# Moving steps in the drain order of a fused window attention and MLP kernel

## The chip, the cores and the metric

The kernel runs on one core of a Trainium2 chip, as one launch. The metric is the device time of that launch in microseconds. Three runs of the kernel before took 1027.41 to 1027.53 us, with a median of 1027.45 us.

## The reference

Two stages, in float32 and float64. The first is a causal window over 7 positions whose weights come from a softmax; the second is a two-layer MLP with a SiLU between.

```python
# x: (4, 4096, 192); weight_gen: (4, 4096, 8, 7); group = 192 // 8
w = weight_gen - max(weight_gen, axis=-1); w = exp(w); w = w / (sum(w, axis=-1) + 1e-09)
x_pad = concatenate([zeros((B, 6, D)), x], axis=1)
out = einsum('bshk,bskhg->bshg', w, x_unf)       # x_unf[b, s, k] = x_pad[b, s + k], as heads of 24
# the MLP: x is out as (16384, 192), w_in (192, 2048), w_out (2048, 192), both float64
h = x @ w_in
g = h * (1.0 / (1.0 + exp(-h)))
return (g @ w_out).astype(float32)
```

## The kernel before, in words

**Tiles.** The 16384 tokens are 128 partitions by 128 rows. Four rows make a block (512 tokens): 32 blocks, b = 0 to 31. Inputs arrive by chunks: chunks 0 and 1 are one block each, chunk 2 is two blocks, chunks 3 to 9 are four blocks each. The 2048 hidden values are 8 pairs p of 256.

**What each engine does for a block.**
- Window: seven products of shifted x with a softmax weight and their sums (`prep_steps`, lines 496 to 525; a product is line 508, a sum line 514). In a folded block GpSimd makes products 0 to 3 and adds them, VectorE makes 4 to 6, and `addpool` joins the two sums. GpSimd's steps are timed by the table row `fold_p`, VectorE's by `fold_v` (block 7: `fold_1`).
- Split: ScalarE rounds the scaled result to float16 (line 481), VectorE takes the rest (line 484), so that float16 matmuls keep precision. A transposing DMA and two swapping DMAs on the queue SP put both halves into `xt` and `xu` (lines 488 to 492, 476).
- First matmul (`mm1`, line 741; folded: line 677) into pairs of PSUM banks. ScalarE applies SiLU in place (line 753) and writes the upper half of the hidden values (`upper`, line 764); VectorE writes the rest (`lower`, line 768). Only after `lower` may TensorE write those banks again.
- Second matmul (line 782, from block 6 on lines 807 and 811) into other banks, and the output: in a folded block `finish_sums` (lines 700 to 709), which is one ScalarE instruction (line 705), a wide add (line 706) and a small add (line 707) on GpSimd, and for every second row tile a store on SP.

**Folding.** From block 7 on (`FOLD`), half of the first matmul is replaced by seven smaller products on sums of rows (`fold_x`, lines 616 to 643: four small GpSimd steps, ScalarE's and VectorE's halves, one transposing DMA and two swaps) and on differences of the weights (`fold_w`, lines 588 to 614: made once; five pairs of an upper half on ScalarE, line 604, and a lower half on VectorE, line 608). The partial products are put together in PSUM by `keep` on ScalarE (line 693) and four `joined` on VectorE (line 698).

**Once per chunk.** `softmax_steps` (lines 398 to 427): maximum, subtraction, exp, sum (line 416), reciprocal (lines 420 and 421), product. `scale_steps` (lines 429 to 451): sizes of four parts on ScalarE, two DMAs, then on VectorE a reduction over 512 values (line 206) and three instructions on one value a row (`small`, lines 212 and 221), then three more (`finish_scales`, `out_scale`).

**What sets the order.** The order of the instructions of each engine is written out by hand, and each engine works through its own in that order. Around the matmuls the other steps wait in a list `todo` with a due time; `drain(u)` (line 877) issues all with a due time up to u, in the order of due times. A block is 16 units. The due times are rows of the table `START`, added to a base `u0` that for block b is 16(b - 2), and for a chunk the same of its first block. Before folding a drain stands at each unit or so. In the folded loop (lines 1141 to 1177) a half block is 8 units and has drains at 0, 1, 2, 3, 5, 6 and 7 only. In short:

```python
drain(u); fold_1(x); fold_1(y); words(last); keep(); lower(last); joined x 3
drain(u + 1); tile_sums; finish_sums; plain(z); fold_2(x)
drain(u + 2); joined(3, 1, 1); drain(u + 3); tile_sums; words(z); lower(z)
drain(u + 5); fold_3(x); words(x); lower(x)
drain(u + 6); words(y); tile_sums; finish_sums; plain(last); lower(y); drain(u + 7)
```

`words` is SiLU and `upper` on ScalarE; x, y, z and last are pairs of hidden values. `fold_1(x)` needs the `lower` of the x before it, `fold_1(y)` that of the y before it, and `fold_3` the last `joined`.

Of the kernel before, what the change touches and what calls it, by code (L numbers as in the profile page):

```python
# [43 lines left out]
BESIDE = ()  # L44
START = {
    "b2v": (13.1,) * 1 + (13.2,) + (13.3,) * 3 + (13.4,) * 4 + (13.45,) + (19,) + (21,) * 2 + (23, 23, 23),
    "first_s": (-2, 1, 4, 6.2, 6.5, 8.5),
    "first_x": (-4, -1, 1, 9, 9.25, 18, 19, 20),
    "any_s": (-32, -32, -23, -15, -14, -10),
    "c4s": (-32, -32, -19, -16, -13, -10),  # L50
    "any_x": (-39, -31, -13, -5.5, -4.0, 13.5, 13.5, 15),
    "early": (-5, -41),
    "b3v": (11, 11, 13, 13, 15, 17, 17, 18, 19, 20.5, 20.5, 21, 21, 22.5, 23, 23),
    "b4v": (10, 12, 13, 14.5, 16, 17, 18.5, 20, 22.5, 23, 23),
    "any_p": (11.25,) * 5,
    "any_v": (11, 11.5, 13, 14, 15, 17, 18.5, 20, 22.5, 23, 23),
    "fold_1": (9, 9, 11, 13, 14, 14, 14, 19, 19),
    "fold_v": (5, 7, 9, 11, 12.5, 14.5, 17, 19, 19),
    "fold_p": (0.5, 3.5, 5, 7, 9, 11, 14),
    "fold_s": (14.5, 16.5, 16.5, 16.5, 18, 23, 23),  # L60
    "fold_w": (36, 58, 60, 62, 66, 81, 81, 84, 86, 87, 88, 90, 93, 94, 95),
    "prep": (12.5,),
    "load": (0,),
}
# [1159 lines left out]
```

## Time and profile before

| | |
|---|---|
| profiled execution, its own time | 1027.18 us |
| its span, first to last instruction | 1025.4 us |
| TensorE matmuls (PE) busy | 1011.7 us, 99% |
| VectorE (DVE) busy | 851.7 us, 83% |
| ScalarE (ACT) busy | 823.6 us, 80% |
| GpSimd (POOL) busy | 627.6 us, 61% |
| granted TensorE clock | 1.000 over the span |
| share of PE in the chain that ended last | 90% |

Busy is the time in which an engine worked on at least one instruction. Matmuls overlap one another, so PE busy is no measure of how fast it goes. The folded part begins at 234 us. A row of a timeline gives the start and the length in us, engine, line, operation, what it writes and reads, and in brackets how long the engine had been idle and what ended that.

### The profile page before, as it was taken

The numbers are of one execution on the slowest core, as the hardware profiler recorded it, in microseconds if no ns is written. First come the engines' busy times: TensorE is split into PE (matmuls) and PEld (weight loads), VectorE is DVE, ScalarE is ACT, GpSimd is POOL, SyncE is SP. The second block draws the span as 40 slices with busy tenths as digits, with TensorE's granted clock in tenths as the row PEclk, the third lists the DMA queues.
The fourth block names the chain that finished last, engine by engine and source line by source line (L and its number), as shares of the span: only waits on it lengthen the run. The fifth ranks groups of instructions, "written<-read, shape, count | busy, mean of one in ns | idle before, by whom it ended". The sixth has DMA issues, their size and how long they took to land.

```text
span 1025.4 us, 32480 instructions
## 1 busy us (share of the span) xinstructions
PE 1011.7 (99%) x14392; PEld 732.4 (71%) x14392; DVE 851.7 (83%) x905; ACT 823.6 (80%) x875; POOL 627.6 (61%) x525
## 2 busy tenths in 40 slices
PE   9999999999999999999999999999999999999998
PEld 7699777677777766677667776677666776666666
DVE  8898877978898888889889889888888988889553
ACT  7988668767898779877898878988789878778774
POOL 1000553555887777786687677887687876777220
PEclk9999999999999999999999999999999999999999
DMA  9542511225213352124432143233422321223200
GB/s 247 157 130 73 167 33 48 58 53 170 49 40 76 61 171 59 46 53 111 121 69 58 47 153 69 61 68 63 142 54 68 71 68 45 47 54 67 63 17 25
DMA packets 105351, 82.91 MB, mean 81 GB/s; under 512 B 79869, under 2 KB 94842, under 8 KB 104186
## 3 DMA queue, kind: packets, MB, share of 16 engines
q1 hardware_dynamic: 105210, 80.84, 31.3%
q8 instruction: 112, 1.84, 0.8%
q14 instruction: 29, 0.24, 0.1%
HBM read 29.68 MB, written 12.60 MB: 41 GB/s over the span
## 4 chain that ended last, share of the span: by engine, by line
PE 90%; DVE 6%; ACT 2%; issue 1%; DMA 0%; DVEq 0%; ACTq 0%
PE banks L741 26%; PE banks L807 24%; PE banks L677 16%; PE banks L811 12%; PE banks L782 6%; PE banks L732 2%; PE banks L794 2%; DVE ringed L768 2%; DVE banks L698 1%; ACT banks L753 1%; ACT ringed L764 1%; DVE pr L508 1%; PE banks L555 1%; DVE ws L416 1%; DVE xv L698 0%
## 5 line engine op out<-in xcount | busy, mean ns | idle before, releaser
L807 PE MATMUL banks<-wo,ringed 64*128 64x384 f16 x3312 | 419.8, 322 | 0.0
L811 PE MATMUL banks<-wo,ringed 64*128 64x192 f16 x3312 | 407.7, 243 | 0.1
L768 DVE SCALAR_TENSOR_TENSOR ringed<-banks,gup,ringed 128x1024 f16<-128x1024 f32 x248 | 315.9, 1277 | 68.3 <-ACT ringed L764 68.2
L753 ACT ACTIVATE banks<-banks,inv 128x1024 f32<-128x1024 f32 x248 | 269.1, 1085 | 97.6 <-PE banks L741 81.2
L764 ACT ACTIVATE ringed<-banks,gup 128x1024 f16<-128x1024 f32 x248 | 276.1, 1113 | 8.0
L508 POOL TENSOR_TENSOR pr<-xc,wc 128x768 f32<-128x768 f32 x109 | 192.0, 1764 | 91.4 <-DVE wc L424 58.9
L807 PEld LDWEIGHTS <-ringed 64*128 64x128 f16 x3312 | 177.8, 94 | 89.3
L741 PEld LDWEIGHTS <-w 64*128 64x128 f16 x2664 | 149.9, 94 | 114.9 <-issue 4.8
L706 POOL TENSOR_TENSOR v_in<-v_in 128x384 f32<-128x384 f32 x100 | 106.1, 1061 | 193.9 <-ACT v_in L705 193.9
L741 PE MATMUL banks<-xt,w 64*128 64x512 f16 x1332 | 185.0, 376 | 3.5 <-DVE ringed L768 3.3
L741 PE MATMUL banks<-xu,w 64*128 64x512 f16 x1332 | 184.9, 376 | 0.0
L811 PEld LDWEIGHTS <-ringed 64*128 64x128 f16 x3312 | 177.7, 94 | 6.3 <-DVE ringed L768 0.4
L514 POOL TENSOR_TENSOR pr<-pr,pr 128x768 f32<-128x768 f32 x81 | 177.2, 2188 | 6.3
L698 DVE TENSOR_TENSOR banks<-banks,xv 128x512 f32<-128x512 f32 x150 | 104.0, 694 | 80.2 <-PE banks L677 74.7
L508 DVE TENSOR_TENSOR pr<-xc,wc 128x768 f32<-128x768 f32 x108 | 150.6, 1398 | 0.2
L705 ACT ACTIVATE v_in<-banks,od 128x768 f32<-128x768 f32 x100 | 89.6, 896 | 70.1 <-PE banks L811 54.2
L677 PE MATMUL banks<-xu,w 64*128 64x256 f16 (+1 forms) x600 | 135.0, 322 | 3.5 <-DVE ringed L768 3.5
L677 PE MATMUL banks<-xt,w 64*128 64x256 f16 (+1 forms) x600 | 135.0, 322 | 0.0
L677 PEld LDWEIGHTS <-w 64*128 64x128 f16 x1500 | 103.9, 94 | 29.5
L514 DVE TENSOR_TENSOR pr<-pr,pr 128x768 f32<-128x768 f32 x105 | 120.2, 1145 | 0.6
L677 PEld LDWEIGHTS <-v_in 64*128 64x128 f16 x1200 | 86.3, 94 | 27.6 <-issue 6.3
L677 PE MATMUL banks<-v_out,v_in 64*128 64x256 f16 x900 | 99.3, 269 | 0.0
(122 smaller groups left out, 960.6 us busy)
## 6 DMA issues: line engine op xcount, KB each, us to landing
xc<-in_x_dram SPq DMA_DIRECT2D x7, 2112.0 KB, 9.6
xu<-xt SPq DMA_DIRECT2D x62, 192.0 KB, 2.9
out_dram<-o SPq DMA_DIRECT2D x61, 192.0 KB, 1.9
v_out<-v_out SPq DMA_DIRECT2D x50, 128.0 KB, 2.3
wc<-in_weight_gen_dram SPq DMA_DIRECT2D x7, 448.0 KB, 3.7
ringed<-in_moe_w_out_dram SPq DMA_DIRECT2D x8, 384.0 KB, 8.7
ringed<-in_moe_w_in_dram SPq DMA_DIRECT2D x14, 192.0 KB, 8.4
ml_x<-line_x SPq DMA_DIRECT2D x7, 256.0 KB, 4.1
```

The costliest lines, as they stand in the source:

```text
L508: eng.tensor_tensor(out=pr[k].rearrange("p t (h g) -> p (t h) g", g=G), in0=xin, in1=wv, op=ALU.mult)
L514: eng.tensor_tensor(out=pr[k], in0=pr[k], in1=pr[l], op=ALU.add)
L677: nc.tensor.matmul(h, w, x, start=start, stop=False, skip_group_check=True)
L698: nc.vector.tensor_tensor(out=to, in0=quarter[:, :, in0], in1=kept[:, :, in1], op=ALU.add)
L705: nc.scalar.activation(out=s, in_=banks[:, 4:6, 0:2 * D], func=AF.Copy, scale=sc[c, "od"])
L706: nc.gpsimd.tensor_tensor(out=s[:, 0], in0=s[:, 0], in1=s[:, 1], op=ALU.add)
L741: nc.tensor.matmul(h[:, i], w16[rows, part, p, g], x_in[rows, :, k, :], start=n == 0, stop=n == NT9 - 1)
L753: nc.scalar.activation(out=h, in_=h, func=AF.Silu, scale=sc[chunk_of[b], "inv"])
L764: nc.scalar.activation(out=g_t[b, p][:, 0], in_=h_t[b, p], func=AF.Copy, scale=sc[chunk_of[b], "gup"])
L768: nc.vector.scalar_tensor_tensor(out=g[:, 1], in0=h_t.pop((b, p)), scalar=sc[chunk_of[b], "gup"], in1=g[:, 0], op0=ALU.mult, op1=ALU.subtract)
L807: nc.tensor.matmul(acc_t[b, t, i], gh_t[b, f][rows, t * P:(t + 1) * P], wo16[rows, place(f)], start=f == 0, stop=False, skip_group_check=True)
L811: nc.tensor.matmul(acc_t[b, t, i][:, 0, :], gl_t[b, f][rows, t * P:(t + 1) * P], wo16[rows, place(f), 0], start=False, stop=False, skip_gr ...
```

## The change

Nine rows of the table `START` get other numbers; no instruction is added or taken away, and no other line changes.

```diff
-    "first_s": (-2, 1, 4, 6.2, 6.5, 8.5),
-    "first_x": (-4, -1, 1, 9, 9.25, 18, 19, 20),
-    "any_s": (-32, -32, -23, -15, -14, -10),
-    "c4s": (-32, -32, -19, -16, -13, -10),
-    "any_x": (-39, -31, -13, -5.5, -4.0, 13.5, 13.5, 15),
+    "first_s": (-2, 0, 4, 5.2, 7.5, 8.5),
+    "first_x": (-9, -1, 2, 9, 9.25, 18, 19, 20),
+    "any_s": (-32, -32, -23, -16, -14, -10),
+    "c4s": (-32, -31, -19, -16, -13, -10),
+    "any_x": (-39, -31, -13, -5.5, -4.0, 12.5, 12.5, 15.5),
...
-    "fold_1": (9, 9, 11, 13, 14, 14, 14, 19, 19),
+    "fold_1": (9, 9, 11, 13, 14, 14, 14, 20, 20),
...
-    "fold_p": (0.5, 3.5, 5, 7, 9, 11, 14),
-    "fold_s": (14.5, 16.5, 16.5, 16.5, 18, 23, 23),
-    "fold_w": (36, 58, 60, 62, 66, 81, 81, 84, 86, 87, 88, 90, 93, 94, 95),
+    "fold_p": (0.5, 3.5, 5, 7, 9, 9, 14),
+    "fold_s": (14.5, 16.5, 16.5, 16.5, 18, 23, 25),
+    "fold_w": (36, 58, 60, 62, 66, 81, 81, 84, 86, 87, 87, 87, 94.5, 94.5, 95),
```

What becomes of the order in which the engines get their instructions:
- `any_x` (chunks 4 to 9): on VectorE the reduction and `small` go from behind the `lower` of x in a second half block to ahead of the sum that stands before that `lower`; the last chain of the scale goes from the last drain of a half block to the first of the next. For chunk 4 the same swap with a sum falls just before the folded part.
- `any_s` (chunks 5 to 9): the softmax sum goes from behind three `joined` to ahead of the `lower` of last.
- `fold_p` (blocks 9 to 31): GpSimd's fourth product goes from behind the two adds of `finish_sums` to ahead of them, in 23 second half blocks.
- `fold_s`: the transposing DMA of the row sums and its two swaps go from the last drain of a first half block to the second drain of the second half block.
- `fold_w`: of the conversions of the weight sums, the third lower half goes ahead of VectorE's split of block 6, the fourth behind the `lower` of pair 7 of block 5; ScalarE's fourth upper half goes up to the third, and its fifth behind the split of block 7.
- `first_s`, `first_x`, `c4s`, `fold_1`: steps of chunks 3 and 4 and the end of block 7's split, by one drain or by a place within one.

## Rows read from the trace of the kernel before

**Rows 1.** Waits of PE: who waited, for whom, us, times, longest

```profile
PE banks L677 <- DVE ringed L768: 3.5, 5, 0.7
PE banks L741 <- DVE ringed L768: 3.3, 4, 2.1
PE banks L677 <- DVE banks L698: 1.1, 5, 0.2
```

**Rows 2.** Timeline of PE: first matmuls of half blocks, and the late group at 358.64

```profile
295.44 0.27 PE L677 MATMUL banks<-xt,w 64*128 64x256 f16 x1
...
311.16 0.27 PE L677 MATMUL banks<-xt,w 64*128 64x256 f16 x1
...
341.79 0.27 PE L677 MATMUL banks<-xt,w 64*128 64x256 f16 x1
...
357.10 0.27 PE L677 MATMUL banks<-xt,w 64*128 64x256 f16 x1
...
358.64 0.27 PE L677 MATMUL banks<-xu,w 64*128 64x256 f16 x1 [0.71 <-DVE ringed L768]
...
373.31 0.27 PE L677 MATMUL banks<-xt,w 64*128 64x256 f16 x1
```

**Rows 3.** Timeline of VectorE, second half block before a chunk boundary

```profile
347.75 0.95 DVE L514 TENSOR_TENSOR pr<-pr,pr 128x768 f32<-128x768 f32 x1
...
350.44 2.10 DVE L508 TENSOR_TENSOR pr<-xc,wc 128x768 f32<-128x768 f32 x1
352.46 1.27 DVE L768 SCALAR_TENSOR_TENSOR ringed<-banks,gup,ringed 128x1024 f16<-128x1024 f32 x1
353.66 1.37 DVE L514 TENSOR_TENSOR pr<-pr,pr 128x768 f32<-128x768 f32 x1
354.95 1.27 DVE L768 SCALAR_TENSOR_TENSOR ringed<-banks,gup,ringed 128x1024 f16<-128x1024 f32 x1
356.14 0.67 DVE L206 TENSOR_REDUCE ra_x<-ml_x 128x1 f32<-128x512 f32 x1
...
357.30 1.28 DVE L768 SCALAR_TENSOR_TENSOR ringed<-banks,gup,ringed 128x1024 f16<-128x1024 f32 x1
```

**Rows 4.** Timeline of GpSimd in the same half block

```profile
346.00 1.80 POOL L514 TENSOR_TENSOR pr<-pr,pr 128x768 f32<-128x768 f32 x1
...
349.63 0.60 POOL L707 TENSOR_TENSOR o<-v_in 128x192 f32<-128x192 f32 x1
350.19 1.54 POOL L508 TENSOR_TENSOR pr<-xc,wc 128x768 f32<-128x768 f32 x1
351.80 2.41 POOL L514 TENSOR_TENSOR pr<-pr,pr 128x768 f32<-128x768 f32 x1
357.01 0.99 POOL L706 TENSOR_TENSOR v_in<-v_in 128x384 f32<-128x384 f32 x1 [2.80 <-ACT v_in L705]
```

**Rows 5.** Timeline of ScalarE in the same half block: the `upper` of y

```profile
355.03 1.11 ACT L764 ACTIVATE ringed<-banks,gup 128x1024 f16<-128x1024 f32 x1
```

**Rows 6.** Timeline of VectorE, first half block with a softmax sum

```profile
297.94 1.28 DVE L768 SCALAR_TENSOR_TENSOR ringed<-banks,gup,ringed 128x1024 f16<-128x1024 f32 x1 [0.76 <-ACT ringed L764]
...
301.26 1.08 DVE L416 TENSOR_REDUCE ws<-wc 128x128 f32<-128x896 f32 x1
```

**Rows 7.** Busy time by windows, the stretch before folding: length, then each engine

```profile
195.00:210.20 15.20, 12.12 (x198) 8.81 (x194) 14.95 (x14) 9.86 (x12) 9.17 (x8) 1.00 0.26 71
```

**Rows 8.** Timeline of PE, late first matmuls in that stretch

```profile
202.97 0.39 PE L741 MATMUL banks<-xt,w 64*128 64x512 f16 x2 [2.06 <-DVE ringed L768]
...
210.20 0.39 PE L741 MATMUL banks<-xt,w 64*128 64x512 f16 x2 [0.66 <-DVE ringed L768]
```

**Rows 9.** Timeline of VectorE in that stretch

```profile
192.84 0.62 DVE L841 SCALAR_TENSOR_TENSOR o<-banks,od,t 128x384 f32<-128x384 f32 x1 [1.00 <-ACT t L840]
...
195.69 1.32 DVE L608 SCALAR_TENSOR_TENSOR v_in<-v_out,w_up,v_in 64x256 f16<-64x256 f32 x1
...
205.42 0.48 DVE L608 SCALAR_TENSOR_TENSOR v_in<-v_out,w_up,v_in 64x256 f16<-64x256 f32 x1
```

## The prediction

> **What bounds the kernel now.** I read the list of waits first, then the order of time on TensorE, then the engines around each wait. The page has PE busy for 99% of the span, so time can come only from moments in which PE stands still, or from a new one. The list of waits has three kinds after the start-up [rows 1]: 3.5 us in five waits of the folded matmuls (line 677) for a `lower` of VectorE (line 768), 1.1 us in five waits for a `joined` (line 698), and 3.3 us in four waits of the plain first matmul (line 741) for a `lower`. Five, five and a cluster: the fives are once per chunk.
>
> The idle times are too small as a measure, because matmuls overlap. The starts of half blocks tell more [rows 2]: 357.10 - 341.79 = 15.31 us in an ordinary one, but 373.31 - 357.10 = 16.21 us after the second half before a chunk boundary, and 311.16 - 295.44 = 15.72 us where the wait for `joined` lies. So the idle 0.71 us costs 0.90 and the idle 0.22 us costs 0.41. Five of each: 6.5 us. The second matmul group of `fold_1` would have started at 358.64 - 0.90 = 357.74 [rows 2].
>
> For the cluster, the row of a window shows who is the bound: from 195.0 to 210.2 us VectorE is busy 14.95 of 15.20 us while PE falls to 12.12 [rows 7]. The waits are 2.06 at 202.97 and 0.66 at 210.20 [rows 8]; the other two of the four are 3.3 - 2.7 = 0.6 in sum.
>
> **The change part by part.**
>
> *Scale of the next chunk (`any_x`, 13.5 to 12.5).* The reduction and three small instructions (`top`, `small`) stand on VectorE between the `lower` of x (354.95) and that of y (357.30), so they push the latter by 357.30 - 356.14 = 1.16 us [rows 3]. After the change they stand ahead of the sum at 353.66. VectorE has no idle time from 350.44 on, so this move by itself saves nothing of the 1.16 us; what it changes is whom the sum meets. That sum took 1.37 us against 0.95 for the same size at 347.75 [rows 3], since GpSimd's add (351.80 to 354.21) was still running [rows 4]; 1.16 us later it is alone: 0.42 us saved. The end of the chain for the chunk (15 to 15.5) goes from the last drain of one half block to the first of the next; nothing of VectorE lies between, so its order is the same: nothing.
>
> *GpSimd's fourth product (`fold_p`, 11 to 9).* It goes ahead of the two adds of `finish_sums`, 23 times. First how the two engines disturb each other. The product at 350.44 on VectorE took 2.10, 1.15 over 0.95; GpSimd's product (350.19, 1.54) still had 1.29 to run. GpSimd's add at 351.80 took 2.41, 0.61 over the 1.80 at 346.00; VectorE's product had 0.74 to run. The sum at 353.66 took 0.42 more, with 0.55 left of GpSimd's add [rows 3, 4]. So the second to start waits for the first to end, less 0.13 us, three times alike; the `lower`s (1.27 and 1.28) are not touched.
> Now the half block at the boundary with the new order. The product starts after 346.00 + 1.80 + 0.08 = 347.88; VectorE's sum runs until 348.70, so it is 0.82 - 0.13 = 0.69 longer and ends at 347.88 + 1.54 + 0.69 = 350.11. The wide add (0.99 alone, the row at 357.01) runs from there to 351.10. VectorE's product at 350.44 waits 0.66 - 0.13 = 0.53 and ends at 351.92 instead of 352.54: 0.62 saved. GpSimd's small add (0.60) waits behind it to 352.39, and the last add (1.80) ends at 354.15, before the sum begins at 354.19. So: `lower` of z 351.84 to 353.11, the reduction and small ones to 354.19, sum to 355.14, `lower` of x to 356.33, `lower` of y to 357.53 (each starts 0.08 before the one ahead ends, as in rows 3; ScalarE's half of y is there at 355.03 + 1.11 = 356.14 [rows 5]). The release took 0.06 (358.58 to 358.64), so PE may go at 357.59, and wants to at 357.74. The 0.90 us vanish with 0.15 to spare: 5 x 0.90 = **4.5 us**. Bounds: 0.42 x 5 = 2.1 if only the sum is spared, 4.5 above. Late next is nothing in that half: `lower` of x ends 0.77 before the 357.10 at which x is wanted. In the other 18 second halves VectorE only gets earlier, and the adds that go later feed the output store alone.
> The Trainium skill (SBUF — State Buffer, § Who interferes with whom) says that the pair of ports which the two engines share is an exclusive lock, and that the loser "fully blocks". The rows say the same but for the 0.13. By the rule in full, GpSimd's product ends at 350.24, VectorE's at 352.14, the last add at 354.50, and the `lower` of y lets PE go at 357.90: 0.16 late, 0.8 us over five chunks, so the sum would be 0.8 smaller and the time 1019.6. I take the rows.
>
> *Sum of the softmax (`any_s`, -15 to -16), five chunks.* The reduction of 1.08 us (301.26) goes ahead of the `lower` at 297.94, before which VectorE idles 0.76 us for ScalarE [rows 6]. So that `lower` and the joins behind it are up to 1.08 - 0.76 = 0.32 later, and what stands ahead of the late `joined` is 0.76 us less. It was 0.41 us late: gone, with about 0.35 to spare. 5 x 0.41 = **2.0 us**; bounds 0 (if the 0.32 hits the plain matmul that waits for the same `lower`) and 2.05.
>
> *Weight sums' conversions (`fold_w`).* The lower half at 195.69 (1.32 us) goes ahead of the split of block 6, before the idle 1.00 us at 192.84; the one at 205.42 (0.48) goes behind the `lower` that PE waits for at 210.20 [rows 8, 9]. That takes 1.32 + 0.48 = 1.80 us out of the stretch in which VectorE is the bound. The two products behind the first then start earlier and meet GpSimd's terms at other points, which I can't place to better than some tenths; for that I add 0.3: **2.1 us**. Bounds: 0, if the moved conversion pushes the two output steps behind it by as much as it took, and 4.0, all of the 3.3 idle with some 0.18 more for each of the four, as the folded wait showed. ScalarE's upper halves move with them; no wait of PE names ScalarE [rows 1], so they are priced at nothing, and inside the bounds just given.
>
> *The rest.* `first_s`, `first_x` and `c4s` move the third chunk's subtraction, its sum and two of ScalarE's sizes by one place, in blocks 1 and 2, well before the cluster. Outside the cluster line 741 waits for at most the 0.6 us left over above, so the `lower`s there have slack and the price is nothing; if it weren't covered, two steps of some 1.08 (the row of the reduction, [rows 6]): 2.2 us lost. `fold_s` (23 to 25) issues a transposing DMA and two swaps one half block's edge later, but on SP they have the same neighbours (output store ahead, next output store behind), and the sums they feed are read half a block later: nothing. `fold_1` likewise keeps its order on VectorE and SP.
>
> Sum: 4.5 + 2.0 + 2.1 = 8.6 us. The profiled execution took 1027.18 (span 1025.4 and 1.8 around it), so 1018.6; the median of the runs is 0.27 above it: **1018.8 us**.
>
> **Rivals.** (B) *The waits at the boundary only shorten.* GpSimd's adds move onto VectorE's product, and it stays at 2.10: then 2.1 + 2.0 + 2.1 = 6.2 us, 1021.2. For it: three of GpSimd's instructions now crowd into 350.1 to 354.2; against: VectorE's product started second before too, and with more left ahead of it.
> (C) *The cluster gives nothing*, because the 1.00 us gap is taken by the split meeting GpSimd's add: 4.5 + 2.0 = 6.5 us, 1020.9.
> (D) *Slower: GpSimd keeps its place in front.* If both adds of `finish_sums` and the last add all go ahead of VectorE's product, it ends at 350.11 + 0.99 + 0.08 + 0.60 + 1.80 + 0.82 = 354.4 instead of 352.54. An ordinary second half has 1.16 - 0.90 = 0.26 us of slack, so it decides from a product of 2.36 us on; at 354.4 each of 18 loses 1.86 - 0.26 = 1.6 us, the five at boundaries 1.86 - 0.42 = 1.4 more than now. 28.8 + 7.2 - 4.1 = +32 us: 1059. Against it: the last add let VectorE's waiting product go first (350.44 before 351.80).
> (E) *Nothing that counts moves.* The work of VectorE ahead of each late `lower` is the same but for contention, and if the overlaps come back elsewhere the time stays: 1027.4.
>
> **How the numbers follow.** Forecast 0.57, B 0.15, C 0.14, E 0.07, D (or a small loss of that kind) 0.07. A measurement of this kernel can tell about 0.2%, 2.1 us. Faster takes forecast, B and C: 0.86; same is E: 0.07; slower is D: 0.07. The range goes from 1017.0, close to the case in which the cluster gives all of its 4.0, to 1022.5, past B and C and most of what an uncovered third chunk adds; B and C together (1023.3) stay outside.
>
> **What would show it.** Half blocks all at 15.31 us, also those of 16.21 and 15.72, with no wait on line 677; VectorE's product at 1.4 to 1.6 instead of 2.10 in 23 second halves and the sum behind it at 0.95; the 2.06 us wait at 203 us mostly gone. A product of 2.4 or more, or waits of line 677 in ordinary second halves, would make the forecast wrong, as would new waits of line 741 in blocks 1 and 2.

## The result, and the profile after

The changed kernel takes 1018.75 us (median of 4 runs, 1018.70 to 1018.76) against 1027.49 us for the kernel before in the same comparison (4 runs, 1027.41 to 1027.54). The ratio is 0.9915 with a 95% interval of 0.9898 to 0.9932: 8.74 us, or 0.85%, faster. The forecast was 1018.8. The span of the profiled execution fell by 8.4 us (1025.4 to 1017.0). The granted clock is 1.00 in both profiled executions, which is the 2.4 GHz level, so these 8.4 us are work and waits alone. The other 0.3 us are clock, as e5 shows.

The list of what PE waited for comes first again (who waited and for whom, us in total, times, longest). It answers to [rows 1].

```profile
PE banks L741 <- DVE ringed L768: 1.0, 3, 0.4
PE banks L907 <- DVE zero L893: 1.0, 1, 1.0
PE banks L570 <- DVE ringed L564: 0.7, 1, 0.7
```

The five waits of line 677 for a `lower` and the five for a `joined` are gone, and the 3.3 us of line 741 are 1.0. So is a wait of 0.2 us for line 841 (at 232.28) that [rows 1] does not show. The other two rows are from the start-up. The timeline of PE shows it by periods, the answer to [rows 2]: the starts of half blocks in the first two chunks that are folded.

```profile
293.44 0.27 PE L677 MATMUL banks<-xt,w 64*128 64x256 f16 x1
308.76 0.27 PE L677 MATMUL banks<-xt,w 64*128 64x256 f16 x1
...
339.38 0.27 PE L677 MATMUL banks<-xt,w 64*128 64x256 f16 x1
354.69 0.27 PE L677 MATMUL banks<-xt,w 64*128 64x256 f16 x1
370.01 0.27 PE L677 MATMUL banks<-xt,w 64*128 64x256 f16 x1
```

308.76 - 293.44, 354.69 - 339.38 and 370.01 - 354.69 are 15.31 to 15.32 us each, where before there were three lengths, 15.72, 15.31 and 16.21. All others of the folded part take 15.31 us too, except its first (15.53). So PE now sets the pace there.

The half block that ends at a chunk boundary, on VectorE (start, length, line, operation), answers to [rows 3]; between the reduction and the sum lie small instructions only.

```profile
348.02 1.44 DVE L508 TENSOR_TENSOR pr<-xc,wc 128x768 f32<-128x768 f32 x1
349.38 1.27 DVE L768 SCALAR_TENSOR_TENSOR ringed<-banks,gup,ringed 128x1024 f16<-128x1024 f32 x1
350.57 0.67 DVE L206 TENSOR_REDUCE ra_x<-ml_x 128x1 f32<-128x512 f32 x1
...
351.74 0.94 DVE L514 TENSOR_TENSOR pr<-pr,pr 128x768 f32<-128x768 f32 x1
352.59 2.47 DVE L768 SCALAR_TENSOR_TENSOR ringed<-banks,gup,ringed 128x1024 f16<-128x1024 f32 x2
```

And GpSimd in the same stretch, which answers to [rows 4]:

```profile
345.47 2.22 POOL L508 TENSOR_TENSOR pr<-xc,wc 128x768 f32<-128x768 f32 x1
347.65 0.99 POOL L706 TENSOR_TENSOR v_in<-v_in 128x384 f32<-128x384 f32 x1
348.72 1.18 POOL L707 TENSOR_TENSOR o<-v_in 128x192 f32<-128x192 f32 x1
349.87 1.81 POOL L514 TENSOR_TENSOR pr<-pr,pr 128x768 f32<-128x768 f32 x1
```

The product is 1.44 us instead of 2.10; the sum is 0.94 instead of 1.37, since GpSimd's last add ends at 349.87 + 1.81 = 351.68, just before it begins. The `lower` of y ends at 352.59 + 2.47 = 355.06. PE wants it at 354.69 + 0.64 (358.64 - 0.90 - 357.10 in [rows 2]) = 355.33; with the release of 0.06, 0.2 us are to spare.

In the stretch before folding the order of VectorE reads as follows, from the moved conversion on (for [rows 9]).

```profile
190.76 0.48 DVE L608 SCALAR_TENSOR_TENSOR v_in<-v_out,w_up,v_in 64x256 f16<-64x256 f32 x1
191.28 2.46 DVE L484 SCALAR_TENSOR_TENSOR xs<-pr,xup,xs 128x768 f16<-128x768 f32 x1
...
195.91 4.24 DVE L508 TENSOR_TENSOR pr<-xc,wc 128x768 f32<-128x768 f32 x2
```

GpSimd there:

```profile
187.69 3.22 POOL L508 TENSOR_TENSOR pr<-xc,wc 128x768 f32<-128x768 f32 x2 [18.04 <-DVE pr L514]
190.99 1.93 POOL L514 TENSOR_TENSOR pr<-pr,pr 128x768 f32<-128x768 f32 x1
```

The first matmuls of PE that were late before [rows 8]; the idle time before one stands in brackets. The second answers to one at 205.44 that waited 0.36 us.

```profile
201.40 0.39 PE L741 MATMUL banks<-xt,w 64*128 64x512 f16 x2 [0.29 <-DVE ringed L768]
203.62 0.39 PE L741 MATMUL banks<-xt,w 64*128 64x512 f16 x2
208.16 0.39 PE L741 MATMUL banks<-xt,w 64*128 64x512 f16 x2 [0.44 <-DVE ringed L768]
```

And the window of the same length (length, then PE, PEld, VectorE, ScalarE and GpSimd busy, the granted clock, DMA share, GB/s), which answers to [rows 7].

```profile
193.00:208.20 15.20, 14.27 (x218) 10.27 (x216) 15.03 (x14) 10.33 (x13) 11.87 (x8) 1.00 0.40 96
```

VectorE is as full as before (15.03 of 15.20), but PE does 14.27 us of work in the window instead of 12.12. The matmul that began at 210.20 now begins at 208.16, 2.04 us earlier, of which 0.11 were there ahead of this stretch (the late matmul at 184.97 is at 184.86).

### The profile page after: what moved, and what is told of

Read it like the earlier page. It is cut to its first block, busy times and chain, and to the rows that moved or that the text cites. A ratio compares the mean times of both kernels' runs of the same rounds, so it can differ in the third digit from the quotient of the medians.

```text
span 1017.0 us, 32485 instructions
## 1 busy us (share of the span) xinstructions
PE 1011.0 (99%) x14392; PEld 710.2 (70%) x14392; DVE 849.2 (84%) x905; ACT 822.2 (81%) x875; POOL 638.6 (63%) x525
## 3 DMA queue, kind: packets, MB, share of 16 engines
q8 instruction: 112, 1.84, 0.8%
## 4 chain that ended last, share of the span: by engine, by line
PE 96%; DVE 2%; ACT 1%; issue 1%; DVEq 0%; ACTq 0%
PE banks L741 27%; PE banks L807 26%; PE banks L677 18%; PE banks L811 13%; PE banks L782 6%; PE banks L732 2%; PE banks L794 2%; DVE ringed L768 1%; DVE pr L508 1%; PE banks L555 1%; PE banks L907 1%; ACT banks L753 0%; ACT ringed L764 0%; DVE pr L514 0%; PE banks L820 0%
## 5 line engine op out<-in xcount | busy, mean ns | idle before, releaser
L508 POOL TENSOR_TENSOR pr<-xc,wc 128x768 f32<-128x768 f32 x109 | 208.2, 1912 | 93.9 <-DVE wc L424 57.9
L807 PEld LDWEIGHTS <-ringed 64*128 64x128 f16 x3312 | 162.0, 94 | 104.6
L706 POOL TENSOR_TENSOR v_in<-v_in 128x384 f32<-128x384 f32 x100 | 99.4, 994 | 180.8 <-ACT v_in L705 180.8
L811 PEld LDWEIGHTS <-ringed 64*128 64x128 f16 x3312 | 161.8, 94 | 7.7 <-DVE ringed L768 0.5
L514 POOL TENSOR_TENSOR pr<-pr,pr 128x768 f32<-128x768 f32 x81 | 162.2, 2002 | 4.5
L508 DVE TENSOR_TENSOR pr<-xc,wc 128x768 f32<-128x768 f32 x108 | 136.2, 1265 | 0.2
L514 DVE TENSOR_TENSOR pr<-pr,pr 128x768 f32<-128x768 f32 x105 | 130.5, 1243 | 0.7
L707 POOL TENSOR_TENSOR o<-v_in 128x192 f32<-128x192 f32 x100 | 95.0, 950 | 7.8
```

The lines of the kernel that those rows point to most:

```text
L508: eng.tensor_tensor(out=pr[k].rearrange("p t (h g) -> p (t h) g", g=G), in0=xin, in1=wv, op=ALU.mult)
L514: eng.tensor_tensor(out=pr[k], in0=pr[k], in1=pr[l], op=ALU.add)
L706: nc.gpsimd.tensor_tensor(out=s[:, 0], in0=s[:, 0], in1=s[:, 1], op=ALU.add)
L707: nc.gpsimd.tensor_tensor(out=o[:, t], in0=s[:, 0, 0:D], in1=s[:, 0, D:2 * D], op=ALU.add)
L807: nc.tensor.matmul(acc_t[b, t, i], gh_t[b, f][rows, t * P:(t + 1) * P], wo16[rows, place(f)], start=f == 0, stop=False, skip_group_check=True)
L811: nc.tensor.matmul(acc_t[b, t, i][:, 0, :], gl_t[b, f][rows, t * P:(t + 1) * P], wo16[rows, place(f), 0], start=False, stop=False, skip_gr ...
```

## The experiments

The theory: three independent gains. **Boundary** (`any_x` with `fold_p`): in the five half blocks before a chunk boundary VectorE meets GpSimd for less long, 4.5 us. **Sum** (`any_s`): the softmax sum runs in idle time, 2.0 us. **Conversions** (`fold_w`): 1.8 us of VectorE's work leave the stretch in which it is the bound, 2.1 us. The rest: nothing. The rivals are those of the prediction, and in addition that the two rows of the boundary each give their own part, whether or not the other is there. Each edit is to the kernel before unless it says otherwise.

**The scale alone (e1).**

```diff
-    "any_x": (-39, -31, -13, -5.5, -4.0, 13.5, 13.5, 15),
+    "any_x": (-39, -31, -13, -5.5, -4.0, 12.5, 12.5, 15.5),
```

> The kernel before with the row any_x alone changed (the reduction of the next scale ahead of VectorE's sum). Theory, the two engines take turns: VectorE's work ahead of the late lower stays the same, only the sum is spared GpSimd's add (0.42 us), so each of the five boundaries is still 0.48 us late: half blocks of 15.79 instead of 16.21, 2.1 us gained, 1025.4. Rival, the place alone decides: the lower of y is free of the 1.16 us, all of 5 x 0.90 goes, 1023.0. Rival, only contention by the product counts: 1027.5.

Measured: 1025.22 us against 1027.47, ratio 0.9979 (0.9970 to 0.9988): 2.25 us. In its VectorE rows the product is as long as before and the sum is free of GpSimd:

```profile
350.83 2.11 DVE L508 TENSOR_TENSOR pr<-xc,wc 128x768 f32<-128x768 f32 x1
...
355.22 0.94 DVE L514 TENSOR_TENSOR pr<-pr,pr 128x768 f32<-128x768 f32 x1
```

The boundary half block takes 15.78 us (16.21 before), and PE still waits there, less long:

```profile
358.60 0.27 PE L677 MATMUL banks<-xu,w 64*128 64x256 f16 x1 [0.27 <-DVE ringed L768]
```

So 0.43 us come off the sum five times, the lower bound of the boundary term.

**The fourth product alone (e2).**

```diff
-    "fold_p": (0.5, 3.5, 5, 7, 9, 11, 14),
+    "fold_p": (0.5, 3.5, 5, 7, 9, 9, 14),
```

> The kernel before with the row fold_p alone changed (GpSimd's fourth product ahead of the two output adds). Theory of turns: VectorE's product falls from 2.10 to 1.44, but the sum two places later now begins 0.7 us into GpSimd's last add and waits for it, 1.93 instead of 1.37, so the lower of y comes only about 0.1 earlier: 0.3 to 0.5 us over five boundaries, 1027.1. Rival, the parts add up: 0.62 us at each boundary, 3.1 us, 1024.4. Rival, it costs: stalls in the 18 ordinary second halves, over 1028.

Measured: 1026.93 us against 1027.47, ratio 0.9995 (0.9986 to 1.0004): not told apart from nothing. The product on VectorE is shorter by 0.67, and the sum behind it longer by 0.56 (1.93 for 1.37):

```profile
350.75 1.44 DVE L508 TENSOR_TENSOR pr<-xc,wc 128x768 f32<-128x768 f32 x1
...
353.31 1.93 DVE L514 TENSOR_TENSOR pr<-pr,pr 128x768 f32<-128x768 f32 x1
```

GpSimd's last add tells why. It used to go beside the `lower`, and now begins 0.70 before the sum and has 1.12 left when the sum starts:

```profile
352.61 1.82 POOL L514 TENSOR_TENSOR pr<-pr,pr 128x768 f32<-128x768 f32 x1
```

The contention was moved from one instruction to the next. The five waits of line 677 for a `lower` are 3.0 us in all instead of 3.5, which fits the small gain expected, though the times can't confirm it. The rival by which each row brings its own part (1024.4) falls.

**Both (e3).** The edits of e1 and e2 together.

> The kernel before with any_x and fold_p changed together. Theory of turns: together they clear the five boundaries, 4.5 us, 1023.0, more than the sum of the two alone (2.1 + 0.4). Rival, additive parts: 2.1 + 3.1, cut at 4.5, also 1023.0, but then the second run alone is at 1024.4.

Measured: 1023.03 us, ratio 0.9958 (0.9944 to 0.9973): 4.44 us, where e1 and e2 add up to 2.79. No wait of line 677 for a `lower` is left; the two other kinds are untouched:

```profile
PE banks L741 <- DVE ringed L768: 3.3, 4, 2.1
PE banks L677 <- DVE banks L698: 1.1, 5, 0.2
```

**Without the fourth product (e4).** This kernel leaves GpSimd's fourth product and the sum that adds it out of the folded blocks, so that term is missing from its output. The two lines added put all later lines two further on (770 is 768).

```diff
         pool = ...
+        if fold:
+            pool[5:] = [lambda: None] * 2
```

> The kernel before without GpSimd's fourth product and its sum in all folded blocks (the output lacks that term); no step is moved. Theory of turns: VectorE's product takes 0.95 instead of 2.10 and the sum 0.95 instead of 1.37, 1.57 us saved where 0.90 is late, so the five boundaries are clear: 1023.0. Rival, the place of the reduction decides and GpSimd is no cause: 1027.5.

Measured: 1020.98 us, ratio 0.9939 (0.9922 to 0.9955): 6.5 us, 2 more than expected. The boundary is as expected: product and sum on VectorE at their undisturbed length, and no wait of the folded matmuls for a `lower`.

```profile
348.66 0.95 DVE L508 TENSOR_TENSOR pr<-xc,wc 128x768 f32<-128x768 f32 x1
...
350.86 0.95 DVE L514 TENSOR_TENSOR pr<-pr,pr 128x768 f32<-128x768 f32 x1
```

Most of the other 2 us comes from the stretch before folding, since the first folded matmul starts at 232.25 us instead of 234.03. The terms of block 7 are computed there, also without the fourth, and VectorE's two products at 197.01 meet less of it, 3.35 us in place of the 4.70 of the kernel before. Line 741, here 743, waits 1.6 us in all instead of 3.3:

```profile
197.01 3.35 DVE L508 TENSOR_TENSOR pr<-xc,wc 128x768 f32<-128x768 f32 x2
```

```profile
PE banks L743 <- DVE ringed L770: 1.6, 3, 0.7
```

I had overlooked that the edit reaches there. What it shows is that contention makes up some 1.35 us of that cluster too. The rival by which GpSimd is no cause (1027.5) falls.

**The softmax sum alone (e5).**

```diff
-    "any_s": (-32, -32, -23, -15, -14, -10),
+    "any_s": (-32, -32, -23, -16, -14, -10),
```

> The kernel before with the row any_s alone changed (the softmax sum ahead of the lower of last, five chunks). Theory: half blocks of 15.72 become 15.31, 2.0 us, 1025.4. Rival, the sum delays the lower that the plain matmul waits for: no gain or a loss, 1027.5 to 1029.

Measured: 1025.58 us against 1027.42, ratio 0.9982 (0.9972 to 0.9991): 1.84 us. The half blocks of 15.72 us are 15.31, and the wait for a `joined` is gone from the list:

```profile
PE banks L677 <- DVE ringed L768: 3.6, 5, 0.7
PE banks L741 <- DVE ringed L768: 2.3, 2, 2.1
```

Line 741 has two waits here, where [rows 1] has four. The reason is TensorE's clock: in this execution it fell to its lower level, 1.2 GHz, for 3.4 us after PE had stood still for 2.06 us at 203 (a window as in [rows 7]; 0.50 is the granted clock).

```profile
203.40:206.80 3.40, 3.40 (x19) 1.45 (x17) 3.34 (x4) 0.16 (x1) 0.00 (x0) 0.50 0.22 77
```

PE was then later itself and did not have to wait for the next two `lower`s. In the profiled execution of the kernel before, the clock in that window is 1.00. Of the 25 runs of the kernel before that e5 to e8 are compared with, 15 have a mean clock of 1.000 and a median of 1027.20 us, and 10 have 0.998 and 1027.50; so the fall costs some 0.3 us. Of the 44 runs of e1, e2, e3, e5 and e7, which keep the wait of 2.06 us, 21 have 0.998. Of the 27 runs of e4, e6, e8, e9 and the changed kernel, in which it is shorter, none has. No run changes that wait alone, so that it brings the fall is likely, not shown.

**The conversions alone (e6).**

```diff
-    "fold_w": (36, 58, 60, 62, 66, 81, 81, 84, 86, 87, 88, 90, 93, 94, 95),
+    "fold_w": (36, 58, 60, 62, 66, 81, 81, 84, 86, 87, 87, 87, 94.5, 94.5, 95),
```

> The kernel before with the row fold_w alone changed (two lower halves of the weight sums out of the stretch from 195 to 210 us). Theory: 1.9 to 2.1 us, 1025.5, the wait of 2.06 us at 203 us falls to some 0.3. Rival, the gain before folding came from the other moved rows: 1027.5.

Measured: 1025.29 us against 1027.42, ratio 0.9979 (0.9970 to 0.9989): 2.13 us. The waits of line 741 fall to what the changed kernel has, the others stay:

```profile
PE banks L677 <- DVE ringed L768: 3.6, 5, 0.7
PE banks L677 <- DVE banks L698: 1.1, 5, 0.2
PE banks L741 <- DVE ringed L768: 1.0, 3, 0.4
```

**All the other rows (e7).**

```diff
-    "first_s": (-2, 1, 4, 6.2, 6.5, 8.5),
-    "first_x": (-4, -1, 1, 9, 9.25, 18, 19, 20),
+    "first_s": (-2, 0, 4, 5.2, 7.5, 8.5),
+    "first_x": (-9, -1, 2, 9, 9.25, 18, 19, 20),
-    "c4s": (-32, -32, -19, -16, -13, -10),
+    "c4s": (-32, -31, -19, -16, -13, -10),
-    "fold_1": (9, 9, 11, 13, 14, 14, 14, 19, 19),
+    "fold_1": (9, 9, 11, 13, 14, 14, 14, 20, 20),
-    "fold_s": (14.5, 16.5, 16.5, 16.5, 18, 23, 23),
+    "fold_s": (14.5, 16.5, 16.5, 16.5, 18, 23, 25),
```

> The kernel before with first_s, first_x, c4s, fold_1 and fold_s changed. Theory: nothing, 1027.3 to 1027.6. Rival, they carry part of the gain before folding: up to 2 us, 1025.5.

Measured: 1027.17 us against 1027.42, ratio 0.9997 (0.9988 to 1.0007), with the same three kinds of waits as before. The four parts, each by itself, add up to 4.44 + 1.84 + 2.13 + 0.25 = 8.66 us, against 8.74 for the whole: within the noise they don't depend on each other.

**Two more steps out of the cluster (e8), an edit to the changed kernel.** Three waits of line 741 are left, 0.26 at 184.86, 0.29 at 201.40 and 0.44 at 208.16. The softmax sum of the `c4s` row stands ahead of the first on VectorE, and two sums of terms (2.02 us from 204.88) stand right ahead of the `lower` for which the last one waits. I moved the softmax sum ahead of a product, a `lower` and a sum, and the second of the two sums behind that `lower`.

```diff
-    "c4s": (-32, -31, -19, -16, -13, -10),
+    "c4s": (-32, -31, -19, -18, -13, -10),
-    "fold_1": (9, 9, 11, 13, 14, 14, 14, 20, 20),
+    "fold_1": (9, 9, 11, 13, 14, 14.4, 17, 20, 20),
```

> The changed kernel with two more moves on the late lowers that are left: the fourth chunk's softmax sum two places up (c4s -16 to -18), into an idle 1.86 us of VectorE at 175 us, and the last sum and the upper half of block 7 behind the lower that TensorE waits for at 208 us (fold_1: 14, 14 to 14.4, 17). Theory, VectorE's work ahead of a late lower is the price: 0.43 us at 185 and 0.62 us at 208, 1.0 us, 1017.7. Rival, the next lower is late instead: 1018.8 or more.

Measured: 1020.04 us against 1027.42, ratio 0.9927 (0.9913 to 0.9942): 1.3 us slower than the changed kernel, where 1 us less was expected. The waits at 185 and 208 are gone, but line 741 waits anew at 205.06 (0.36) and 227.05 (0.25), and a new kind stands in the list, for the output steps of line 841:

```profile
PE banks L782 <- DVE o L841: 1.6, 2, 1.1
```

GpSimd's wait for block 7's terms ends with a sum of VectorE on `pr` (line 514). With the softmax sum out of the way that sum begins at 186.21 instead of 186.71, and GpSimd at 187.18 instead of 187.69. Its add now comes ahead of the moved conversion:

```profile
190.49 1.81 POOL L514 TENSOR_TENSOR pr<-pr,pr 128x768 f32<-128x768 f32 x1
```

```profile
190.79 1.79 DVE L608 SCALAR_TENSOR_TENSOR v_in<-v_out,w_up,v_in 64x256 f16<-64x256 f32 x1
192.61 2.40 DVE L484 SCALAR_TENSOR_TENSOR xs<-pr,xup,xs 128x768 f16<-128x768 f32 x1
```

The conversion takes 1.79 us instead of 0.48, and the two output steps behind the split come too late for PE.

**Only the second of the two (e9), an edit to the changed kernel.** It tells whether the new waits of e8 came from the earlier start of GpSimd or from the `fold_1` row.

```diff
-    "fold_1": (9, 9, 11, 13, 14, 14, 14, 20, 20),
+    "fold_1": (9, 9, 11, 13, 14, 14.4, 17, 20, 20),
```

> The changed kernel with one of the two further moves: the last sum of block 7 and ScalarE's upper half of it behind the lower that TensorE waits for at 208 us (fold_1: 14, 14 to 14.4, 17); the softmax sum of the fourth chunk stays. Theory: the new waits of the run before came from GpSimd starting 0.5 us earlier on its terms of block 7, not from this move; so here the 0.44 us wait at 208 us goes and nothing comes: some 0.6 us, 1018.1. Rival, this move made the new waits at 195 and 197 us: 1020.

Measured: 1018.84 us (5 runs, 1018.76 to 1019.49) against 1027.49, ratio 0.9917 (0.9904 to 0.9931): the same as the changed kernel, where 0.65 less was expected. The two waits of line 782 aren't there, so in e8 they needed the edit of `c4s`, which is the one that lets GpSimd start earlier; that edit was not run alone. The wait at 208 is gone as expected, but another has come in the next block (and one of 0.2 us for line 841, as the kernel before has it):

```profile
225.90 0.39 PE L741 MATMUL banks<-xt,w 64*128 64x512 f16 x2 [0.49 <-DVE ringed L768]
```

VectorE's product of block 8, 0.95 us long in the changed kernel (at 222.79), starts 0.39 us behind GpSimd's add and takes 2.56:

```profile
222.09 2.56 DVE L508 TENSOR_TENSOR pr<-xc,wc 128x768 f32<-128x768 f32 x1
```

```profile
221.70 2.14 POOL L514 TENSOR_TENSOR pr<-pr,pr 128x768 f32<-128x768 f32 x1
```

GpSimd comes later than in the changed kernel because the moved sum does: its small steps of line 624 wait for that sum's `pr`, and its products of block 8 stand behind them and start at 210.25 instead of 209.01.

None of the versions run is faster than the changed kernel.

## Why the prediction was right, point by point

**The total, 8.6 us predicted, 8.74 measured.** Between the two profiled executions it is 1027.18 - 1018.75 = 8.43 us. The first folded matmul starts at 231.98 instead of 234.03, so 2.05 us lie ahead of the folded part (predicted 2.1) and 6.4 in it (predicted 6.5). The forecast then added 0.27 us, by which the median of the kernel before lay above its profiled execution. That fits the 0.3 us of the clock's fall (e5), which none of the changed kernel's four runs shows: their median and their profiled execution are both 1018.75. So a gain 0.17 too large and an addition 0.27 too large nearly cancel. That the forecast came within some tenths is its mechanism; that it came within 0.05 is luck.

**The measure.** The prediction counted 0.90 and 0.41 us per half block from periods, not the 0.71 and 0.22 of idle time. Clearing the five boundary waits gave 4.44 us (e3), where five times 0.90 is 4.5 and five times the idle time would be 3.5. Clearing the five joins gave 1.84 (e5), where five times 0.41 is 2.05 and five times 0.22 would be 1.1. Periods were the right measure both times. The 0.41 was read from one half block; the other four of its kind take 15.69 us, so the five are late by 0.41 + 4 x 0.38 = 1.93.

**The boundary, 4.5 us predicted, 4.44 measured.** The step that moves the scale "by itself saves nothing of the 1.16 us; what it changes is whom the sum meets": e1 shows it, with the lower bound of 2.1 us as 2.25. The shorter product was to bring the rest. e2 shows that it can't alone: without the 1.16 us of small instructions ahead of the sum, GpSimd's last add runs into the sum. Together product and sum are 0.66 + 0.43 = 1.09 us shorter, of which PE can use 0.90. That leaves 0.2, where the prediction had 0.15.

**The rule of the two engines.** The prediction had the second to start wait for the first to end, less 0.13 us, read from three rows; it gave 1.48 us for the product, and 1.44 came. With the changed kernel's own rows, the wide add has 347.65 + 0.99 - 348.02 = 0.62 left when the product starts, so the rule in full gives 0.95 + 0.62 = 1.57, and less 0.13 it is 1.44. The new rows carry it further: in e2 the sum has 1.12 us of the add ahead, so 0.95 + 1.12 - 0.13 = 1.94, measured 1.93; in e9 the product has 221.70 + 2.14 - 222.09 = 1.75 ahead, so 2.57, measured 2.56. The Trainium skill (SBUF — State Buffer, § Who interferes with whom) has the loser blocked fully, by which the forecast was 1019.6; the product of 1.44 us stands on the side of the rows. In that forecast the 352.14 is 0.04 too small beside its own 350.24 + 0.99 + 0.95 = 352.18, which makes it 1019.8.

**The miss.** The list of what would show it says "the sum behind it at 0.95" in 23 second halves. That holds in the five boundary halves only. In the other 18 the scale's steps are not there, and it is longer than the 1.37 us of before. In an ordinary second half of the changed kernel VectorE's product and sum are

```profile
317.40 1.45 DVE L508 TENSOR_TENSOR pr<-xc,wc 128x768 f32<-128x768 f32 x1
...
319.96 1.93 DVE L514 TENSOR_TENSOR pr<-pr,pr 128x768 f32<-128x768 f32 x1
```

and GpSimd's last add is

```profile
319.25 1.82 POOL L514 TENSOR_TENSOR pr<-pr,pr 128x768 f32<-128x768 f32 x1
```

The add has 319.25 + 1.82 - 319.96 = 1.11 us left, so the rule that the prediction already had gives 1.93. It worked the sum out for the boundary half and took it over to the others ("In the other 18 second halves VectorE only gets earlier"). It cost nothing: 0.66 saved on the product and 0.56 lost on the sum leave VectorE 0.1 us earlier still, and an ordinary half has slack.

**The softmax sum, 2.0 predicted, 1.84 measured.** The sum runs where VectorE had idled for ScalarE, and the `lower` behind it starts 296.07 - 293.44 = 2.63 us into the half block instead of 297.94 - 295.44 = 2.50: 0.13 later, within the 0.32 that the prediction allowed. There is now more slack than it counted, since VectorE idles 0.88 us for PE before the next join:

```profile
295.08 1.07 DVE L416 TENSOR_REDUCE ws<-wc 128x128 f32<-128x896 f32 x1
296.07 1.27 DVE L768 SCALAR_TENSOR_TENSOR ringed<-banks,gup,ringed 128x1024 f16<-128x1024 f32 x1
...
301.48 0.70 DVE L698 TENSOR_TENSOR banks<-banks,xv 128x512 f32<-128x512 f32 x1 [0.88 <-PE banks L677]
```

**The conversions, 2.1 predicted, 2.13 measured**, or 1027.20 - 1025.29 = 1.91 among runs with a clock of 1.000. But the parts are not as the prediction had them. The conversion that moves ahead of the split shrank from 1.32 to 0.48, while the split grew from 1.10 to 2.46, because it now meets GpSimd's add (190.99). That is what rival C describes, and it happened. It gave back less than C feared: the two products start at 195.91 instead of 197.02, and take 4.24 instead of 4.70. The wait of 2.06 us at 203 became 0.29 at 201.40. That the total came so near to 1.8 + 0.3 is partly luck: the prediction's bounds were 0 and 4.0, and it had no part for the clock.

**The rest** is not told from nothing (e7), as predicted.

**The rivals.** B falls with the product of 1.44 us; C's cause was there, its price wasn't; D falls with the order on GpSimd, where the small add (348.72, 1.18 instead of 0.60) already lets VectorE's waiting product (348.02) go first, and the last add (349.87) comes behind both; E falls with the periods.

## What to carry to other kernels

Count a loss that recurs by the distance between like starts, not by the idle time in front of one instruction. Where two engines take turns on one resource, moving an instruction mostly moves the wait to the next one: work the turn out for each kind of stretch that the move touches, and expect that two moves pay only together. Where such stretches have no slack, a gain of some tenths upstream shifts the other engine's whole sequence, so a further "free" move has to be checked on everything behind it. And before tenths are credited to a move, compare runs with the same granted clock.

## What was not expected of the hardware

Idle time on PE understates what a late operand costs: 0.71 us idle lengthened the half block by 0.90, 0.22 idle by 0.41, and clearing them gave these back. The small scaling of 128x128 elements on VectorE took 0.66 us while GpSimd's wide add ran (before) and 0.22 us alone (after):

```profile
302.37 0.66 DVE L420 TENSOR_SCALAR ws<-ws 128x128 f32<-128x128 f32 x1
299.39 0.22 DVE L420 TENSOR_SCALAR ws<-ws 128x128 f32<-128x128 f32 x1
```

None of the 248 `lower`s, with one operand in PSUM, took more than 1.29 us, whatever GpSimd did, while the conversions and splits of the same operation, with operands in SBUF, went from 0.48 to 1.79 and from 1.10 to 2.46. That the place of the operands makes the difference was not tested by itself.
